# Sinkhorn of batch 0 on its own with row sums on TensorE, whole k mixes for batch 0, and fewer weight bytes in flight

## The chip, the cores and the metric

The kernel runs on one core of a Trainium2 chip. A core has five engines with a queue of instructions each, which run in order: TensorE (PE: matmuls into PSUM, and the loads of their stationary operand), VectorE (DVE), ScalarE (ACT), GpSimd (POOL) and SyncE (SP). They meet at semaphores. DMAs are issued here from POOL (loads that cast fp32 to bf16) and from SP (stores, round trips through DRAM, transposes). The metric is the device time of one execution in microseconds; lower is better.

## The reference

Four batches, 8 heads, 768 tokens in 8 blocks of 96, head dimension 64. `sort_net` gives an 8x8 matrix for each batch and head. It goes through five Sinkhorn rounds, the blocks of k and v are mixed by it, each block of q attends to the mixed block of its place, and the result goes through a bilinear feed-forward net.

```python
for _ in range(5):
    P = P - np.max(P, axis=-1, keepdims=True)
    P = np.exp(P)
    P = P / (np.sum(P, axis=-1, keepdims=True) + 1e-09)
    P = P / (np.sum(P, axis=-2, keepdims=True) + 1e-09)
k_sorted = np.einsum('bhij,bhjcd->bhicd', P, k_b)      # v in the same way
scores = scale * q_b @ k_sorted^T                      # within a block
attn = softmax(scores);  x = attn @ v_sorted           # 3072 x 512
out = ((x @ w_a) * (x @ w_b)) @ w_out                  # 512 -> 1536 -> 512
```

## The kernel before

The program is not written in the order in which it runs. Each piece of work is given to `add` with its engine, a guessed duration, what it depends on, and the buffers and PSUM banks that it takes and gives back. `Plan.solve` places the pieces by a string, `ORDER`, that names them one after another, and `emit` writes the instructions of each engine in that order. So the order on each engine is fixed, and an instruction that has to wait holds all that stand behind it on its engine. `_fill` then puts matmuls that nobody reads (line 1222) into the gaps that the plan leaves on TensorE up to 32.6 us.

What the change touches:

- **Sinkhorn** (lines 490 to 504). All 32 matrices lie on 32 partitions, 64 numbers each (`p_nat`). A round is one exponential on ACT (L492) and six DVE steps (L494 to L502): sum, reciprocal and multiply along the rows, then along the columns. The maximum is not subtracted; it cancels in the division. After five rounds the result is repeated 16 times (two copies, one on DVE and one on ACT), turned onto 128 partitions by eight matmuls (L517), and multiplied with a mask into `s_all` (L522), the matrix that mixes blocks. DVE writes `s_all` of batch 0 from PSUM; `p_col` (L533) keeps the rest, from which POOL writes `s_all` of batches 1 to 3, 2.03 us each.
- **Batch 0** goes pair of heads by pair of heads (p = 0 to 3) and in two halves of four blocks each, h = 0 for all pairs first. For each: q is transposed on TensorE (L555), k and v are mixed by matmuls with `s_all` (L582, in halves of 64 columns), v is transposed (L641), scores (L660), exponential on ACT (L665), product with v (L675), division (L681, L686), transpose of the result (L694) into `xT`. A copy out of PSUM, on ACT or DVE, follows each step on TensorE.
- **The first product**, `xT` with w_a and w_b, for batch 0 is L836; its first half needs half 0 of all four pairs. Later batches mix k and v whole (L571, or L619 for v), and use a seven-product scheme for the first product (L930). The second product is L987.
- **Loads** are issued by POOL in one fixed order: for each pair of batch 0 a half of q, k, v (loads 0 to 11), then w_a and w_b block 0, the four other halves of q, then w_a and w_b blocks 2, 1, 3 (loads 12 to 23; a block of w is 384 columns, 0.79 MB), then batch 1, w_out, and so on. `load` makes one wait for an earlier one where more than 2.8 MB would be on their way.
- **q of batch 3** (`QDMA`) is transposed by DMA, issued from SP; that of other batches on TensorE.

Of the kernel before, what the change touches and what calls it, by code (L numbers as in the profile page):

```python
# [9 lines left out]
FP32 = mybir.dt.float32  # L10
# [26 lines left out]
class Plan:  # L37
# [178 lines left out]
    def _fill(self):  # L216

        t, ops = self.warm_from.end + 0.1, sorted((o for o in self.ops if o.eng == "PE"), key=lambda o: o.start)
        for o in ops:
            if o.start > self.warm_until:  # L220
                break
            rate = 2350.0 if t > 8.5 else 1180.0
            cols = int((o.start - t - (0.25 if 8.0 < t < 13.0 else 0.1)) * rate)
            if cols >= 64:
                w = Op({"PE": 0.0}, lambda cols=cols: self.warm_fn(cols), [], [], [], 0.0, None, -1)
                w.eng, w.start, w.end = "PE", t, t + cols / rate
                self.ops.append(w)
            t = max(t, o.end)
# [4 lines left out]
    b"%z1C$e###%#'#)#+#/#-#1#5$g$i#7#;$k$m#A$o#=$q$s#G#3$u$w#C#M$y%^${#I$}#9#S%`%#%%#Y%'#O#?%)%+"  # L233
    b"#`#E%-%/#U#f%1%~%3#[#K%5#l&$%7%9#b#r%;#Q%=#W%?#x%A#h%C&@%E#n#^%G&B%I%K#t%M#d#~%O%Q%S#j$(#z"
    b"%U$.&_#p%W&a%Y$4%b%f#v%d$:%[$$&&%h&H)/&(%j&K%n%l&D&*#|%p&G&2$*&L&-&c$@&4$0%r&O&.)+$6%t&e&P"
    b"&1&g$<$&%v&R&o$B$,&j')&q$2'%$F',&T$8''&k&V'-$L$>&X&m&6&}$H)-'0&Z'#'f&8%x&^'^'h&:'b%|'j$D'a"
    b"&<'d$R$N&s'm'C&>&u'?-j'E&w'n'A'G(($J'p'J($$T'O(+$X'K(&'1'N'Q&y-r'|&|(,'3$P(#*0(/$Z*<$_*@-l"
    b"*>$V$a*2*D*B(>*8*4*F(D$]'S(@*6(J-_*H(P(F*:*T(V$c*J(L-Z(](B*V-c*P(c(R'U*L-e*](i(H*m'W(X-f*N"
    b"(N*X(_*R(T*o(o(e(0-i*u*a(u(Z-](k*Z(2({-a(a,8)%*_(q(4,:*c-v(g(6'Y(w*i(8*e(m+f'](}-p*g+i(s(:"
    b")''5*k(<*q(y)1+n'7*s'9)3)7+q)#'r)=*w';+r'=))-n-1+t't+j'v,4+l)9'x,<,7-t'z+v,>,]-3--)5,`+x,D"  # L240
    b")C,@-0,F-x*})?,C*y+z*{)I);+|+~+))O+%,H)E++)U,J,L,N)[)K+1+#)b)A+-,P+')Q)h,$)G+/,&)n)W+A+3)M"
    b")t,()^+C,*)S)z,e,,+I+5)d,g)Y*$+9)j+7,i)`**.Z+=)p,k,R.^+;)f,T+Y,V)v)l.c+?+M)|)r+[.e+O+b*&.g"
    b"+E)x,m+U/1*,.i+G/3)~,a+K,o-5,c*(+^-7+Q*..k,{-9,q,}+S.m+`,s+W-;._,.,00.+d.a/Y0*00,X/].y,2.o"
    b"0-.{,u.P,w.q-=,y,Z-?-#-A-%/^-'-C.(1E-)/`/5-+-K/7/--M.*/0/9.s.,/b.u/A.w../;-z/C/d/f.0/=/K-O"
    b"/M.}/h-Q-|/#/?.R/%-~02.T-E.$04.<-G-I06/j.&-S.V0>.>080@/E.A/O/l-U.2/G/Q.X/I.B/S-W/x0H0:/z/n"
    b".F.D/p0<0J1H/r/|/t1r/~/v.H1t.41I1v0$.J1L1z.6.L1x1M1|0B25.81~1O0D.N2$0F1U2&1Q.:1W2*2(1[1S26"
    b"202,1^221l1Y2.1`1b282:1h0L2<1j1d1n0N2>0P2B1f0V2D0X0]2@2_0c2H0_2a1q2F2Y2J2g0e0i2N0Z2c2i0o2L"
    b"2e0u0a2m2T0k2[2P2o2V0{2k0q2R2q1%0g4P0w2s4T2]2y3'0m4V2{3#2u3)0s3+4R2}2w3/1+3-4X313K0}0y4Z33"
    b"5#3M3%351'3S114]3F371-3O5%173U3;1#391=3Y3Q3A1)3=3[3C3G3W3?4e4_3j3^1/4g3`5O133z3I6L3f3h3l19"
    b"4a5Q4F151?1;3b6$4c/'0&3d4o6&3|3o5W4q/)5'5Y4H0(5)5S1A4#5[4<4J5|/+5U4L5^5d5~5+5f6(4$5-4(6*4N"  # L250
    b"5/5`4&6,4i/U4*514k574m4,5n5b4>0R594s6.4A425p/W4u534w4B0T646044664.5h55475r3p6N4D485j5t6S5l"
    b"625v6{405;6Q6}3r4:5=7#5?3t7'7%3v687)6V6T7+6:6X7>7-3x6<6_7/6Z6a73716e6]7?79756g7;6u6c776i6k"
    b"7A7C6q6>7E6s6w6m7G6@6o7K7I6y6B7M7h6D7O7c7j7Q6F7p7S7l7r7W7U7v7n7d7^7Y7x7`8*7t7[7z7|5A7f8&80"
    b"5C8(8,7~82848$5E88868.8T8:5G8<8O8V8>5I8]8@8X8_8D8B8c8Z8P8J8F8e8L8s8a8H8y8i8R8v9O8k9;4y5K8m"
    b"8x4{5M8g9'5x8o9Y4}8q6H5z8{9)8}9E6J9,9#9[9-919%9^9`9/9b9d939f9G969Q9I9l979T9h9n:u9U9j9=99:w"
    b"9r:'9K9?9p9W9t:y9A:}9x9M9v;#:{:(9z9~;'9C;79|;%;):$:*:,;-;+:.:0;:;3:4:2;/:6;5:J:8;1::;<;=:<"
    b";A;?:@:>;C:L;E:F:B;[:H;G;I:D;K:O:P;M:T:R;Q;O:V;^:X;W;S;Y:Z:o:];U:_;a;b:a;f;d:e:c;h:q;j:k:g"
    b":m;l<$;n:i;p:t<4;r;v<';t<H;|;~;x<R;z<)<J<T<L<6<W<><N<8<:<P<]<X<<<@<_<Z<B<*<b<D<c<,<F<.<0<e"
    b"<2"
)  # L260
STRASSEN_OUT = ()
QDMA = lambda b, p: b >= 3
VDMA = lambda b, p: 4 * b + p >= 6


@with_exitstack
def kernel(
# [94 lines left out]
    p_col = const.tile([P, NB, BH], BF16, name="p_col")  # L362
    p_nat = const.tile([BH, NB, NB], FP32, name="p_nat")
    ident = const.tile([P, P], BF16, name="ident")
    mask = const.tile([P, CG], BF16, name="mask")
    rsum = const.tile([BH, NB], FP32, name="rsum")
    csum = const.tile([BH, NB], FP32, name="csum")
    p_fin = const.tile([BH, NB, NB], BF16, name="p_fin")
# [9 lines left out]
    def load(fn, nbytes, deps=(), get=(), rank=0.0, many=0.0, spare=0.4):  # L378

        ds, way, behind = [d for d in deps if d is not None], nbytes, None  # L380
        for k in reversed(range(len(ld_n))):
            way += ld_n[k][1]
            if way > 2.8e6 and len(ld_n) < 24 and behind is None:
                behind = ld_i[k]
                ds.append(ld_n[k][0])
        if len(ld_n) >= 7:
            ds.append(ld_n[-7][0])
        i = add("POOL", 0.72 + many, fn, ds + ld_i[-1:], get=get, rank=rank, lat=0.0)
        i.behind = behind
        ld_i.append(i)  # L390
        d = add("DQ", nbytes / RATE, None, [i], rank=rank)
        ld_n.append((d, nbytes))
        return add("NIL", 0.0, None, [d], lat=spare)

    def sp_dma(issue, work, fn, deps, get=(), put=(), rank=0.0, lat=1.5):
        i = add("SP", issue, fn, deps, get=get, rank=rank, lat=0.6)
        return add("DH", work, None, [i], put=put, rank=rank, lat=lat)

    o_p = add("SP", 0.6, lambda: nc.sync.dma_start(
        out=p_nat, in_=sort_net.rearrange("b h i j -> (b h) i j")), lat=1.58)  # L400
# [9 lines left out]

    def pads():
# [7 lines left out]
    o_pads = add("DVE", 1.0, pads, [o_mask], rank=1)  # L419
# [68 lines left out]

    last = o_p
    o_rep = add("NIL", 0.0, None, get=[("o", "p_rep")], rank=-20)  # L490
    for it in range(5):
        last = add("ACT", 0.26, lambda: nc.scalar.activation(out=p_nat, in_=p_nat, func=AF.Exp),  # L492
                   [last], rank=-9)
        last = add("DVE", 0.21, lambda: nc.vector.reduce_sum(out=rsum, in_=p_nat, axis=AX.X),  # L494
                   [last], rank=-9)
        last = add("DVE", 0.19, lambda: nc.vector.reciprocal(out=rsum, in_=rsum), [last], rank=-9)
        last = add("DVE", 0.21, lambda: nc.vector.tensor_mul(
            out=p_nat, in0=p_nat, in1=_ap(rsum, 0, [[NB, BH], [1, NB], [0, NB]])), [last], rank=-9)
        last = add("DVE", 0.26, lambda: nc.vector.reduce_sum(
            out=csum, in_=p_nat.transpose([0, 2, 1]), axis=AX.X), [last], rank=-9)  # L500
        last = add("DVE", 0.19, lambda: nc.vector.reciprocal(out=csum, in_=csum), [last], rank=-9)
        last = add("DVE", 0.21, lambda it=it: nc.vector.tensor_mul(  # L502
            out=p_fin if it == 4 else p_nat, in0=p_nat,
            in1=_ap(csum, 0, [[NB, BH], [0, NB], [1, NB]])), [last], rank=-9)

    def p_rep(i, n):
        return _ap(buf("p_rep").bitcast(BF16), i * NB * CG, [[2 * DMODEL, BH], [NB * CG, n], [1, NB * CG]])

    reps = [add(e, d, lambda h=h, e=e: copy(
        ENG[e], p_rep(h * NBH, NBH).rearrange("p i (j c) -> p i j c", j=NB),  # L510
        _ap(p_fin, h * NBH * NB, [[NB * NB, BH], [NB, NBH], [1, NB], [0, CG]])), [last, o_rep], rank=-9)
        for h, e, d in ((0, "DVE", 0.42), (1, "ACT", 0.62))]

    def spread_ops():
        t = buf("pc")[:, 0:NB * BH].rearrange("p (j h) -> p j h", j=NB)
        for i in range(NB):
            nc.tensor.matmul(t[:, i, :], lhsT=p_rep(i, 1).rearrange("p i k -> p (i k)"),  # L517
                             rhs=ident[0:BH, 0:BH], start=True, stop=True)
    o_pc = add("PE", 0.36, spread_ops, reps + [o_ident], get=[("bank", "pc")], put=["p_rep"], rank=-9)

    def spread(eng, src, h0, n):
        eng.tensor_tensor(  # L522
            out=s_all[:, h0:h0 + n],
            in0=_ap(mask, 0, [[CG, P], [0, n], [0, NB], [1, CG]]),
            in1=_ap(src, h0, [[src.ap[0][0], P], [1, n], [BH, NB], [0, CG]]), op=ALU.mult)

    s_ok = {}
    o = add("DVE", 0.43, lambda: spread(nc.vector, buf("pc"), 0, 2), [o_pc, o_mask], put=["pc"], rank=-9)
    s_ok[0, 0] = o
    o = add("DVE", 0.95, lambda: spread(nc.vector, buf("pc"), 2, 6), [o_pc, o_mask], put=["pc"], rank=-8)  # L530
    for p in range(1, HP):
        s_ok[0, p] = o
    o_col = add("DVE", 0.43, lambda: nc.vector.tensor_copy(  # L533
        out=p_col, in_=buf("pc")[:, 0:NB * BH].rearrange("p (j h) -> p j h", j=NB)), [o_pc],
        put=["pc"], rank=-7)

    def later_spreads(rank):
        for b in range(1, B):
            o = add("POOL", 2.0, lambda b=b: spread(nc.gpsimd, p_col, b * 8, 8), [o_col, o_mask],
                    rank=rank, port=("POOL",))  # L540
# [52 lines left out]
    def mix_half(b, p, what, h, rk, after=None):  # L593
# [9 lines left out]
        return op  # L603

# [96 lines left out]
    def x_dma(b, p):  # L701
        nc.sync.dma_start_transpose(
            out=_ap(buf(("xT", b)), p * S, [[KA * S, P], [BLK, NB], [1, BLK]]),
            in_=buf(("xp", b, p)).rearrange("q i e d -> q (i e d)"))

# [455 lines left out]
    for p in range(HP):  # L1161
        rk = float(p)
        qd = q_part(0, p, 0, rk)
        kd = mix_half(0, p, "k", 0, rk)
        vd = v_part(0, p, 0, mix_half(0, p, "v", 0, rk + 0.05), rk + 0.1)
# [6 lines left out]
    for p in range(HP):  # L1172
# [3 lines left out]
        kd = mix_half(0, p, "k", 1, rk, go)  # L1176
        vd = v_part(0, p, 1, mix_half(0, p, "v", 1, rk, go), rk + 1.0)
        m = so_part(0, p, 1, True, kd, qd, vd, rk + 1.0)
        x_part(0, p, 1, m, rk + 2.0)
# [131 lines left out]
```

## Time and profile before

| | us |
|---|---|
| median of 11 runs | 245.57 (243.72 to 247.99) |
| the profiled execution | 246.36 |
| its span, first to last instruction | 244.6 |
| TensorE busy, fillers among it | 232.8 |
| fillers of line 1222 on TensorE | 10.5 |
| DVE, ACT, POOL busy | 152.3, 115.4, 110.5 |
| s_all of batch 0 begins | 14.55 |
| first product matmul begins | 30.64 |
| last matmul ends | 239.9 |

In the profile's lines, "out<-in" are the tiles that an instruction writes and reads, then come its shape and how many were merged; "[0.30 <-PE ps L582]" is idle time before it and what ended that. In a view by windows each engine has its busy time and, in brackets, its instructions; then come the granted TensorE clock, the share of time that DMA engines were busy, and the rate. In the chain of waits each line is a start, a length and the work that set the pace there; "issue" is time in which the engine waited for nothing that the profile shows.

### The profile page before, as it was taken

To read this page: it belongs to the slowest core of one execution; us is meant where nothing else is said; L and a number is where in the kernel's file an instruction comes from. 1 tells how busy PE (TensorE), PEld (TensorE's weight loads), DVE (VectorE), ACT (ScalarE), POOL (GpSimd) and SP (SyncE) were. 2 spreads that over 40 slices of the span, in tenths; PEclk is the share of its full clock that TensorE was granted. 3 is DMA by queue.
4 is the path that set the end of the run, shared out by engine and by line. 5 is a ranking of instruction groups with operands and counts; after the bars stand their busy time and mean duration, and the time that the engine had idled before them with its cause. 6 is when DMAs were issued, how large, how long until landed. Compare 5 with 4: busy or idle time off the path is not lost.

```text
span 244.6 us, 5464 instructions
## 1 busy us (share of the span) xinstructions
PE 232.8 (95%) x2180; PEld 133.3 (54%) x2196; DVE 152.3 (62%) x305; ACT 115.4 (47%) x174; POOL 110.5 (45%) x123
## 2 busy tenths in 40 slices
PE   8798799999999999999999999999999999999992
PEld 3367556676656555565564454655654455555440
DVE  6658517785656466578884464787673458877410
ACT  2267722575447351666662542666720065563110
POOL 8679997999400000539996002373440004433000
PEclk9999979999999999999999999999999999999997
DMA  5999999999995558436999699500053452000066
GB/s 67 173 198 154 190 168 181 169 148 197 201 204 115 83 141 182 89 75 76 142 148 184 128 200 151 137 3 1 0 67 64 86 118 56 0 0 3 0 129 129
DMA packets 50104, 27.88 MB, mean 114 GB/s; under 512 B 28832, under 2 KB 47008, under 8 KB 50080
## 3 DMA queue, kind: packets, MB, share of 16 engines
q0 software_dynamic: 24112, 14.16, 43.6%
q1 hardware_dynamic: 25968, 13.38, 28.0%
q8 instruction: 17, 0.28, 0.5%
q14 instruction: 7, 0.06, 0.1%
HBM read 30.29 MB, written 8.26 MB: 158 GB/s over the span
## 4 chain that ended last, share of the span: by engine, by line
PE 85%; POOL 5%; DMA 4%; issue 2%; ACT 1%; DVE 1%; SPq 0%; ACTq 0%
PE ps L930 29%; PE ps L987 24%; PE ps L836 14%; PE ps L675 3%; PE ps L660 3%; POOL hT L373 2%; PE ps L571 2%; DMA q<-in_q_dram 2%; PE ps L555 2%; PE ps L582 2%; PE ps L1222 2%; DMA vs<-vd 2%; PE ps L641 2%; POOL q L434 1%; PE ps L619 1%
## 5 line engine op out<-in xcount | busy, mean ns | idle before, releaser
L987 PE MATMUL ps<-w_out_sb,hT 128*128 128x512 bf16 x275 | 64.7, 379 | 0.9 <-issue 0.3
L373 DVE TENSOR_TENSOR f<-f,ps 128x768 f32<-128x768 f32 x54 | 49.8, 951 | 22.3 <-PE ps L930 12.2
L373 POOL TENSOR_TENSOR hT<-f 128x384 bf16<-128x384 f32 x35 | 34.4, 1001 | 49.7 <-DVE f L373 49.6
L936 ACT COPY f<-ps 128x768 f32<-128x768 f32 x54 | 42.2, 800 | 30.2 <-PE ps L930 29.9
L987 PEld LDWEIGHTS <-hT 128*128 128x128 bf16 x288 | 26.8, 98 | 29.4
L665 ACT ACTIVATE eT<-ps 96x768 bf16<-96x768 f32 x32 | 24.9, 811 | 17.1 <-PE ps L660 15.2
L373 DVE TENSOR_TENSOR hT<-a,ps 128x384 bf16<-128x384 bf16 x42 | 22.0, 549 | 16.4 <-PE ps L836 12.4
L930 PE MATMUL ps<-tx,ws_a 128*128 128x384 bf16 x108 | 26.4, 326 | 0.1
L930 PE MATMUL ps<-tx,ws_b 128*128 128x384 bf16 x108 | 26.4, 326 | 0.0
L686 DVE TENSOR_TENSOR xp<-ps,rec 96x512 bf16<-96x512 f32 x32 | 21.6, 683 | 0.7
L836 PE MATMUL ps<-xT,w_a_sb 128*128 128x384 bf16 x96 | 19.5, 343 | 0.0
L930 PEld LDWEIGHTS <-ws_b 128*128 128x128 bf16 x144 | 14.1, 98 | 9.3
L836 PE MATMUL ps<-xT,w_b_sb 128*128 128x384 bf16 x96 | 19.0, 330 | 0.0
L930 PEld LDWEIGHTS <-ws_a 128*128 128x128 bf16 x144 | 13.6, 98 | 9.9 <-ACT f L936 0.5
L847 ACT CAST a<-ps 128x768 bf16<-128x768 f32 x12 | 9.3, 800 | 20.6 <-PE ps L836 20.6
L373 POOL TENSOR_TENSOR tx<-xT 128x768 bf16<-128x768 bf16 x2 | 3.3, 1630 | 34.0 <-DMA xT<-xp 34.0
L930 PE MATMUL ps<-xT,w_a_sb 128*128 128x384 bf16 x72 | 17.6, 326 | 0.0
L930 PE MATMUL ps<-xT,w_b_sb 128*128 128x384 bf16 x72 | 17.6, 326 | 0.0
L966 ACT CAST a<-ps 128x384 bf16<-128x384 f32 x18 | 8.6, 478 | 18.9 <-PE ps L930 18.9
L316 ACT COPY o<-ps 128x512 f32<-128x512 f32 x15 | 8.6, 588 | 17.1 <-PE ps L987 16.8
L316 ACT CAST kT<-ps 128x768 bf16<-128x768 f32 (+1 forms) x19 | 12.9, 683 | 7.6 <-PE ps L571 6.6
L318 DVE COPY o<-ps 128x512 f32<-128x512 f32 x9 | 6.2, 690 | 14.2 <-PE ps L987 14.2
(95 smaller groups left out, 329.2 us busy)
## 6 DMA issues: line engine op xcount, KB each, us to landing
out_dram<-o SPq DMA_DIRECT2D x48, 128.0 KB, 2.4
k<-in_k_dram POOLq DMA_DIRECT2D x16, 192.0 KB, 6.1
v<-in_v_dram POOLq DMA_DIRECT2D x16, 192.0 KB, 6.1
vd<-vm SPq DMA_DIRECT2D x10, 192.0 KB, 2.4
vs<-vd SPq DMA_DIRECT2D x10, 192.0 KB, 3.2
q<-in_q_dram POOLq DMA_DIRECT2D x16, 96.0 KB, 5.2
w_a_sb<-in_moe_w_a_dram POOLq DMA_DIRECT2D x4, 384.0 KB, 6.2
w_b_sb<-in_moe_w_b_dram POOLq DMA_DIRECT2D x4, 384.0 KB, 6.3
```

Source lines behind the costliest of these rows:

```text
L316: nc.scalar.copy(out=out, in_=in_)
L373: ENG[eng].tensor_tensor(out=out, in0=in0, in1=in1, op=op)
L660: nc.tensor.matmul(sc[:, e, i * BLK:(i + 1) * BLK], lhsT=kT[e * D:(e + 1) * D, at:at + P], rhs=rhs, start=True, stop=True)
L665: nc.scalar.activation(out=buf(("eT", b, p, h))[:, :, 0:HB], in_=buf(("sc", b, p, h))[0:BLK, :, 0:HB], func=AF.Exp, scale=float(scale))
L675: nc.tensor.matmul(ops_[:, e, i * OW:(i + 1) * OW], lhsT=eT[:, e, i * BLK:i * BLK + P], rhs=vs[:, h * NBH + i, e * OW:(e + 1) * OW], start ...
L686: nc.vector.tensor_tensor(out=_ap(xp, h * NBH * 2 * D, [[NB * 2 * D, BLK], [D, 2], [2 * D, NBH], [1, D]]), in0=_ap(ops_, 2, [[1024, BLK], ...
L836: nc.tensor.matmul(pf[:, u, 0:HW], lhsT=w_sb[:, kc, (m + u) * P:(m + u + 1) * P], rhs=buf(("xT", b))[:, kc, t * HW:(t + 1) * HW], start=(k ...
L847: ea = add("ACT", 0.8, lambda: nc.scalar.copy(out=buf(("a", b, t, m)), in_=buf(("pf", b, t, m, "a"))[:, :, 0:HW]), [ps_["a", 1]], get=[("a ...
L930: nc.tensor.matmul(buf(key)[:, n, 0:HW], lhsT=lf(n, j), rhs=rf(j), start=start and j == 0, stop=j == 1, skip_group_check=not start)
L936: return add("ACT", 0.8, lambda: nc.scalar.copy(out=buf((name, b, g)), in_=buf(kA)[:, :, 0:HW]), [dep], get=[("f", (name, b, g))], rank=rk)
L966: e21 = add("ACT", 0.48, lambda: nc.scalar.copy(out=buf(("c21", b, g))[:, 0, :], in_=buf(kA)[:, 0, 0:HW]), [p4], get=[("a", ("c21", b, g)) ...
L987: nc.tensor.matmul(po, lhsT=hT[:, t * 2 + m // G, m % G, c * P:(c + 1) * P], rhs=w_out_sb[:, m, :], start=(m == 0), stop=(m == KO - 1), sk ...
```

## The change

1. Batch 0's Sinkhorn leaves the common chain. Its matrices lie on 64 partitions (head and row), 8 numbers each. Sums along a row are taken by the instruction that multiplies; sums along a column, over the partitions of a head, by an fp32 matmul with a mask (`m_same`) on TensorE. The row division is carried into the next exponential as a scale. The result is spread onto 128 partitions by one matmul.
2. The other three batches keep the old chain, on 24 partitions, at a late rank: their steps are put between the work on batch 0.
3. k of batch 0 is mixed whole (`WHOLE`), and copied in two halves; v stays in halves. `XDMA` is there and false.
4. Loads 12 to 23 wait where more than 2.0 MB would be on their way.
5. q of batch 2, pairs 2 and 3, is transposed by DMA as well.
6. `ORDER` is another string for the whole program, and the fillers are sized by another table of rates.

```diff
-            rate = 2350.0 if t > 8.5 else 1180.0
+            rate = 2350.0 if t > 12.4 else 1500.0 if t > 4.65 else 1180.0
...
-QDMA = lambda b, p: b >= 3
+QDMA = lambda b, p: 4 * b + p >= 10
+XDMA = lambda p: False
+WHOLE = lambda p, what: what == "k"
...
-            if way > 2.8e6 and len(ld_n) < 24 and behind is None:
+            if way > (2.8e6 if len(ld_n) < 12 else 2.0e6) and len(ld_n) < 24 and behind is None:
...
+    o_p0 = add("SP", 0.6, lambda: nc.sync.dma_start(
+        out=pa[:, 0, :], in_=sort_net[0].rearrange("h i j -> (h i) j")), lat=1.58)
     o_p = add("SP", 0.6, lambda: nc.sync.dma_start(
-        out=p_nat, in_=sort_net.rearrange("b h i j -> (b h) i j")), lat=1.58)
+        out=p_nat, in_=sort_net[1:B].rearrange("b h i j -> (b h) i j")), [o_p0], lat=1.5)
...
+    def sk_rows():
+        nc.tensor.matmul(buf(bank)[0:HN, NB:2 * NB], lhsT=m_same.rearrange("p h j -> p (h j)"),
+                         rhs=pa[:, 1, :], start=True, stop=True)
...
+    for it in range(4):
+        x = step("ACT", 0.3, lambda it=it: nc.scalar.activation(
+            out=pa[:, 1, :], in_=px if it else buf(bank)[0:HN, 0:NB], func=AF.Exp, scale=pc1), [x], lat=0.2)
+        x = step("PE", 0.12, sk_rows, [x, o_same])
+        x = step("DVE", 0.2, lambda: nc.vector.reciprocal(out=pr, in_=buf(bank)[0:HN, NB:2 * NB]),
+                 [x], put=[bank], lat=0.1)
+        x = step("DVE", 0.2, lambda: stt(px, pa[:, 1, :], 1.0, pr, ps1), [x], lat=0.02)
+        x = step("DVE", 0.15, lambda: nc.vector.reciprocal(out=pc1, in_=ps1), [x], lat=0.1)
...
+    def spread_first():
+        nc.tensor.matmul(buf("p0")[:, 0:HN], lhsT=m_rep.rearrange("p j c -> p (j c)"),
+                         rhs=p_end.rearrange("p i h -> p (i h)"), start=True, stop=True)
...
     for it in range(5):
         last = add("ACT", 0.26, lambda: nc.scalar.activation(out=p_nat, in_=p_nat, func=AF.Exp),
-                   [last], rank=-9)
+                   [last, o_p0], rank=12)
...
+    def mix_first(b, p, what, rk):
+
+        if not WHOLE(p, what):
+            return lambda h, r, after=None: mix_half(b, p, what, h, r, after)
+        pe = add("PE", 0.46, lambda: mix_pe(b, p, what),
+                 [(k_in if what == "k" else v_in)[b, p], s_ok[b, p]],
+                 get=[("pair", (what + "m", b, p))], put=[(what + "2", b, p)], rank=rk)
```

## The prediction

> **What bounds the kernel now.** I read the page first, then the windows of the first 40 us, the chain of waits, the timeline of 9 to 31 us, and last the groups of instructions by shape.
>
> ```profile
> span 244.6 us, 5464 instructions
> PE 232.8 (95%) x2180; PEld 133.3 (54%) x2196; DVE 152.3 (62%) x305; ACT 115.4 (47%) x174; POOL 110.5 (45%) x123
> ...
> PEclk9999979999999999999999999999999999999997
> ```
>
> TensorE is busy 95% of the span, so the end is set by TensorE: a change is worth what it takes from TensorE's work or from its useless time. From 33.9 us to its last matmul at 239.9 us it stands still for only 1.5 us in all. The useless time is in front. "Busy" hides it there, because the matmuls of line 1222 are fillers that nobody reads. I sorted TensorE's time by line: of the first 15.06 us, 10.34 are fillers, 2.92 idle and 1.81 useful; of 15.06 to 30.64 us, 12.79 are useful and 2.79 idle or filler.
>
> ```profile
> 14.55 1.29 DVE L522 TENSOR_TENSOR s_all<-mask,ps 128x256 bf16<-128x256 bf16 x2 [2.24 <-PE ps L517]
> ...
> 15.03 0.38 PE L582 MATMUL ps<-s_all,k 128*64 128x64 bf16 x12
> ```
>
> This is the timeline: the first useful k and v matmuls (line 582) start when s_all, the end of the Sinkhorn chain, is there. k and v of pair 0 had landed at 6.4 and 7.4 us.
>
> ```profile
> 28.50 0.22 PE ps L641 x2
> 28.72 1.75 issue
> 30.48 0.37 PE ps L641 x2
> 30.85 6.01 PE ps L836 x28
> ```
>
> The chain of waits: in the middle of one group of transposes TensorE stands still 1.75 us and waits for nothing that the profile shows. Counted in program order, this stop stands at TensorE's instruction 962; two smaller ones (0.28 us at 19.4, 0.29 us at 24.4) stand at 450 and 706. They are 256 apart, and each comes 1.3 us after the end of one packet of the "instruction" queue (packets began at 17.15, 22.08, 28.17 us; 17 of them carry 0.28 MB, so 16 KB each). I read them as TensorE out of instructions.
>
> ```profile
> 30.00:35.00 5.00, 4.53 (x20) 2.45 (x20) 0.42 (x1) 0.05 (x1) 4.98 (x6) 0.66 1.14 161
> ```
>
> The windows (the last three columns are granted clock, DMA share, GB/s): the clock is 0.50 from 30.27 to 33.69 us, right behind that stop. Matmuls filled 3.06 us of it and would need half.
>
> **The change, part by part.**
>
> *First mixing.* Before: 15.06 us. The new chain for batch 0 works on 64 partitions and 8 columns, with one small matmul on TensorE in each round in place of two DVE steps. A round now is Exp (0.26 before), matmul, reciprocal (0.19), multiply (0.21), reciprocal (0.19), with 0.12 from matmul to DVE and 0.03 to 0.04 at the other hops: about 1.2 us and the matmul, against 1.75 measured before. The trace has no matmul in fp32 and no accumulating DVE step. Below, the matmul takes 0.1 us as the shortest groups do; above, all of it eats the gain (that is a rival). But the chain is now in TensorE's queue, behind the q transposes in program order: its third row matmul behind those of pair 1 (landed 9.01), the spreading matmul behind those of pair 2 (landed 11.66, started 11.80). So: 11.80 + 0.38 transposes + 0.40 filler (858 columns at 2,130 per us, from 8 fillers in 1.83 us) + 0.1 + 0.12 + 0.42 first spread + 0.03 = 13.25. Useful work before it is three q groups, 0.53 + 0.38 + 0.38 = 1.3. Useless: 13.25 - 1.3 = 11.95 against 13.25 before (10.34 + 2.92): **1.3 gained**.
>
> *From there to the first product matmul* (line 836 before, at 30.64; 27 groups in the new order). By the old rows the new order has 10.3 us of TensorE work in front of it: whole k mixes at 0.46, half v mixes 0.31, scores 0.28, o 0.26, v transposes 0.17, x 0.17, q 0.30. The other bound is DVE, which now has two of five Sinkhorn rounds of batches 1 to 3 between its copies: two spreads 1.37, two rounds at 1.26 (0.20 + 0.19 + 0.21 + 0.26 + 0.19 + 0.21), four vs copies at 0.417, one vT and three kT at 0.556, four reciprocals 0.81, four xp at 0.682, four xT and one qT at 0.357: 13.1 us up to the last xT that the product needs. From 12.75 without a pause that is 25.9; at the 82% that DVE was busy in 14.55 to 28.60 before, 28.7. ACT's last exponential for it ends near 22.5 by the same rows. I take 26.5, nearer the low end, because the fillers that stand in this stretch are only 2,600 columns (1.2 us) and TensorE's work plus those gives 24.8. Useless: 26.5 - 13.25 - 10.3 = 2.95 against 2.79: **0.2 lost**. The product starts 4.1 us earlier because less stands ahead of it.
>
> *The instruction stop.* The new order has 805 TensorE instructions before the first product matmul, against 966. Stops 450 and 706 remain and are in the 2.95; number 962 falls behind some 28 product matmuls of 0.163 us each (4.6 us) with 3.7 us of other work. The longest refill before took 6.1 us (24.36 to 30.48), so it is covered with 2 us to spare. Without that cover it is 1.75 us again, and the half clock with it. With it the slow stretch goes: **1.5 gained** (3.06 / 2). The Trainium skill, "TensorE: Matmul & The Clock Gate" (Part 1), says the clock falls after an idle window of about 3.4 us; here a stop of 1.75 us was enough, so the row decides. By the page alone the 1.5 would not be there, and the time 1.5 higher. "Runtime: NRT & Kernel Launch" (Instruction fetch mechanics) calls crossing a 16 KiB block "mostly hidden"; the 1.75 us row differs. By the page neither order has stops, and the 0.2 lost becomes some 2 lost.
>
> *k at once*: 4 x (2 x 0.294 - 0.46) = **0.5 gained** (line 582: 4.71 us in 16 groups; line 571: 0.46). *q of batch 2, pairs 2 and 3, by DMA*: two groups of 0.46 leave TensorE, **0.9 gained**. For them SP issues two more transposes (1.3 us each, 4.9 us to landing) and POOL four q loads in place of two. SP's next vd store and output wait behind them; TensorE is 99% busy with other groups at 85 to 120 us, which hides it. If not, some 2 us each.
>
> *The remaining Sinkhorn* delays s_all of batches 1 to 3: POOL wrote it from 17.0 us, now after the spread on TensorE that stands 285 instructions behind the first product, some 14 us later, so near 41 us, and 2.03 us more on POOL behind a w_out load. Batch 1 was first mixed at 45.3. I cost it at nothing; if POOL is late, the mix holds TensorE's queue. SP now loads sort_net in two parts: batch 0 first, nothing behind it hurries.
>
> *2.0 MB on their way* instead of 2.8: of 0.79 MB weight loads two run at once, not three, and w_a and w_b of the first block wait for v of pair 2 (13.63) and k of pair 3 (15.10) in place of an issue at 11.70 and 13.92. Landings before: 18.17 and 21.39, the other six 24.82 to 36.59, 5.6 to 6.3 us after issue. Two at a time at 5.6 us a pair from 21 us on end at 37.8, and POOL's ws sums (1.65 each) stand between: 38 to 39.6. By the work in front of it, the new order needs the last block near 39. Bounds 0 (before, no product waited) and 3 us; I take **0.6 lost**, nearer zero as the first needs (30 us) meet landings of 29 to 30.
>
> Sum: 1.3 - 0.2 + 1.5 + 0.5 + 0.9 - 0.6 = 3.4 us. The profiled execution took 246.36 (span 244.6, and 1.8 around it), 0.8 over the median of the runs: it would become 243.0, and the median 245.57 becomes **242.1**.
>
> **Rivals.**
>
> *Weights decide.* For it: two loads instead of three, and the demand 4 us earlier. Against: DMA moved 190 to 200 GB/s nearly without pause either way. With 3 us of waits instead of 0.6, and the half clock back (1.5): 242.1 + 2.4 + 1.5 = **246.0**, no change.
>
> *The chain gets no shorter.* For it: unpriced fp32 matmuls and accumulations, five crossings to TensorE, fillers that take twice as long where the clock is still 0.50. Against: the wait for q decides, not the chain. First mixing again at 15.06: 242.1 + 1.8 = **243.9**.
>
> *DVE paces the stretch*, the case that ends slower. In 13 to 27 us, 2.5 us of Sinkhorn steps, each waiting for the one before and twice for ACT, stand in DVE's fixed order before copies that TensorE waits for. At 67% busy 13.1 us take 19.6, the first product is at 32.3, 5.8 later than I say: **247.9**. It decides below 71% busy (product after 31.2). For it: DVE's share over the span is 62%. Against: 82% in this stretch before.
>
> **How the numbers follow.** What this measurement can tell from no change is about 0.5%, 1.2 us: faster is below 244.3, slower above 246.8. Forecast 0.64, chain no shorter 0.14 (both faster: 0.78), weights 0.12 (same), DVE 0.10 (slower). Range: the forecast's own is 239.8 (product at 25.9, no weight waits, first mixing 12.9, 0.8 for the new order later on) to 243.6; up to 245.6 it takes in the second case and half of the first.
>
> **What would show it.** First mixing near 13.2; first product near 26.5; no TensorE stop over 1 us and clock 1.00 from 25 to 40 us; no product idle for w_a or w_b for over 0.6 us. A stop above 1.5 us anywhere in 13 to 40 us with the clock at 0.50 behind it makes it wrong, and so does a first product after 29.

## The result, and the profile after

The changed kernel takes 251.28 us (median of 12 runs, 250.19 to 252.33), the kernel before 245.42 (median of 47 runs). The ratio is 1.028, with a 95% interval of 1.026 to 1.031: slower. The forecast was 242.1. The medians are of all executions, while the ratios, here and below, leave out slow ones (those more than 1.5% above the fastest of their kernel), so the two need not agree (251.28 over 245.42 is 1.024).

The page of the changed kernel, its span, the busy time of its engines and the granted clock:

```profile
span 248.8 us, 5358 instructions
...
PE 233.9 (94%) x2115; PEld 131.4 (53%) x2131; DVE 155.8 (63%) x320; ACT 121.8 (49%) x187; POOL 112.3 (45%) x125
...
PEclk9979985999999999999999999999999999999998
```

The dip at the sixth and seventh slice (31 to 44 us) is deeper than the one of before. The timeline of the changed kernel shows what stands there (start, length, engine, line, operation; the kernel's lines have moved: L569 and L574 are the two multiplications of a round of the late Sinkhorn, L388 the sums of weight blocks, L778 the division that gives xp, L933 the first product):

```profile
13.64 0.53 PE L656 MATMUL ps<-s_all,v 128*64 128x64 bf16 x12
...
27.93 0.81 PE L933 MATMUL ps<-xT,w_a_sb 128*128 128x384 bf16 x4
...
28.43 0.21 DVE L569 TENSOR_TENSOR p_nat<-p_nat,rsum 24x64 f32<-24x64 f32 x1
...
29.32 1.65 POOL L388 TENSOR_TENSOR ws_a<-w_a_sb 128x768 bf16<-128x768 bf16 x1
...
30.40 4.63 DVE L574 TENSOR_TENSOR p_nat<-p_nat,csum 24x64 f32<-24x64 f32 x1
...
30.91 0.78 POOL L485 DMA_DIRECT2D w_b_sb<-in_moe_w_b_dram  x1
31.71 3.24 POOL L388 TENSOR_TENSOR ws_b<-w_b_sb 128x768 bf16<-128x768 bf16 x2
...
33.52 0.82 PE L933 MATMUL ps<-xT,w_a_sb 128*128 128x384 bf16 x4 [0.97 <-DMA w_a_sb<-in_moe_w_a_dram]
...
35.68 1.65 POOL L388 TENSOR_TENSOR ws_b<-ws_b,w_b_sb 128x768 bf16<-128x768 bf16 x1
35.82 1.59 DVE L569 TENSOR_TENSOR p_nat<-p_nat,rsum 24x64 f32<-24x64 f32 x1
...
37.34 0.67 DVE L778 TENSOR_TENSOR xp<-ps,rec 96x512 bf16<-96x512 f32 x1
...
38.07 1.46 PE L933 MATMUL ps<-xT,w_a_sb 128*128 128x384 bf16 x4 [3.72 <-DVE xp L778]
```

The first mixing (13.64) and the first product (27.93) are earlier than before (15.03, 30.64). TensorE first stops for 0.97 us, up to the landing of a weight block. The larger loss is on DVE: a multiplication of the late Sinkhorn took 0.21 us at 28.43, and the next, of the same size, takes 4.63 us at 30.40. It ends 0.08 us after POOL's third weight sum (34.95). The one after that, 1.59 us, ends 0.08 us after the fourth (37.33). The xp that batch 0's second half needs stands behind both in DVE's order, and TensorE stands still for 3.72 us. A half clock follows, 35.82 to 42.65 us; TensorE worked 4.58 us of it (38.07 to 42.65) and lost half, 2.3 us. In the windows of the changed kernel (columns as before: TensorE, weight loads, DVE, ACT, POOL, then clock, DMA share, GB/s) DVE looks fully busy, with two instructions:

```profile
30.00:35.00 5.00, 3.38 (x37) 1.73 (x34) 4.88 (x2) 0.94 (x2) 4.98 (x5) 1.00 1.00 136
35.00:40.00 5.00, 1.93 (x13) 0.83 (x14) 4.61 (x11) 1.30 (x3) 4.97 (x5) 0.58 0.82 109
```

The rate has fallen too: 136 and 109 GB/s, where the kernel before moved 161 and 167. Its last six weight blocks landed from 24.82 to 36.59 us, now from 28.28 to 42.72. So there were two suspects: late weights (the new limit) and multiplications that wait for POOL's sums.

### The profile page after: what moved, and what is told of

The parts are those of the page before. It is cut to its first block, busy times and chain, and to the rows that moved or that the text cites. A ratio compares the mean times of both kernels' runs of the same rounds, so it can differ in the third digit from the quotient of the medians.

```text
span 248.8 us, 5358 instructions
## 1 busy us (share of the span) xinstructions
PE 233.9 (94%) x2115; PEld 131.4 (53%) x2131; DVE 155.8 (63%) x320; ACT 121.8 (49%) x187; POOL 112.3 (45%) x125
## 4 chain that ended last, share of the span: by engine, by line
PE 85%; DMA 5%; DVE 3%; issue 3%; POOL 2%; ACT 1%; POOLq 0%; ACTq 0%; DVEq 0%
PE ps L1027 33%; PE ps L1084 25%; PE ps L933 13%; PE ps L767 3%; PE ps L752 3%; DMA q<-in_q_dram 3%; PE ps L645 2%; DMA k<-in_k_dram 2%; DVE p_nat L574 2%; PE ps L629 1%; PE ps L711 1%; PE ps L733 1%; ACT f L1033 1%; DVE p_nat L569 1%; PE ps L786 1%
## 5 line engine op out<-in xcount | busy, mean ns | idle before, releaser
L388 POOL TENSOR_TENSOR hT<-f 128x384 bf16<-128x384 f32 x35 | 34.4, 1000 | 63.0 <-DVE f L388 63.0
L388 DVE TENSOR_TENSOR f<-f,ps 128x768 f32<-128x768 f32 x54 | 50.1, 951 | 17.1 <-PE ps L1027 12.7
L1084 PEld LDWEIGHTS <-hT 128*128 128x128 bf16 x288 | 26.8, 98 | 29.5 <-issue 0.2
L757 ACT ACTIVATE eT<-ps 96x768 bf16<-96x768 f32 x32 | 25.4, 808 | 17.6 <-PE ps L752 17.2
L388 DVE TENSOR_TENSOR hT<-a,ps 128x384 bf16<-128x384 bf16 x42 | 21.8, 547 | 12.4 <-ACT a L1063 5.2
L933 PE MATMUL ps<-xT,w_a_sb 128*128 128x384 bf16 x96 | 20.4, 343 | 4.7 <-DVE xp L778 3.7
L778 DVE TENSOR_TENSOR xp<-ps,rec 96x512 bf16<-96x512 f32 x32 | 21.4, 680 | 0.6
L318 ACT COPY o<-ps 128x512 f32<-128x512 f32 x16 | 9.4, 586 | 24.4 <-PE ps L1084 21.5
L773 DVE RECIPROCAL rec<-ps 96x8 f32<-96x8 f32 x32 | 6.2, 196 | 22.6 <-PE ps L767 22.3
L933 PE MATMUL ps<-xT,w_b_sb 128*128 128x384 bf16 x96 | 19.6, 335 | 0.0
L1027 PEld LDWEIGHTS <-ws_a 128*128 128x128 bf16 x144 | 13.0, 97 | 10.8 <-DVE f L388 2.2
L1027 PE MATMUL ps<-xT,w_a_sb 128*128 128x384 bf16 x72 | 17.6, 326 | 0.0
L1027 PE MATMUL ps<-xT,w_b_sb 128*128 128x384 bf16 x72 | 17.6, 326 | 0.0
L318 ACT CAST kT<-ps 128x768 bf16<-128x768 f32 (+1 forms) x17 | 11.9, 709 | 7.5 <-PE ps L645 7.4
L1027 PEld LDWEIGHTS <-w_b_sb 128*128 128x128 bf16 x108 | 10.6, 98 | 7.0
L1027 PEld LDWEIGHTS <-w_a_sb 128*128 128x128 bf16 x108 | 9.9, 98 | 8.3 <-ACT f L1033 0.8
```

The source lines that it names most:

```text
L318: nc.scalar.copy(out=out, in_=in_)
L388: ENG[eng].tensor_tensor(out=out, in0=in0, in1=in1, op=op)
L757: nc.scalar.activation(out=buf(("eT", b, p, h))[:, :, 0:HB], in_=buf(("sc", b, p, h))[0:BLK, :, 0:HB], func=AF.Exp, scale=float(scale))
L773: nc.vector.reciprocal(out=buf(("rec", b, p, h)), in_=_ap(buf(("op", b, p, h)), 0, [[1024, BLK], [512 + D, 2], [OW, NBH]]))
L778: nc.vector.tensor_tensor(out=_ap(xp, h * NBH * 2 * D, [[NB * 2 * D, BLK], [D, 2], [2 * D, NBH], [1, D]]), in0=_ap(ops_, 2, [[1024, BLK], ...
L933: nc.tensor.matmul(pf[:, u, 0:HW], lhsT=w_sb[:, kc, (m + u) * P:(m + u + 1) * P], rhs=buf(("xT", b))[:, kc, t * HW:(t + 1) * HW], start=(k ...
```

## The experiments

| run | what it is | median us | ratio to before (95%) | longest multiplication | longest TensorE stop in 28 to 45 us |
|---|---|---|---|---|---|
| after | the change | 251.28 | 1.028 (1.026 to 1.031) | 4.63 | 3.72 |
| e1_limit | 2.8 MB again | 244.29 | 0.989 (0.979 to 0.999) | 1.25 | 0.31 |
| e2_early | multiplications forward, not far enough | 251.39 | 1.020 (1.013 to 1.027) | 5.69 | 5.09 |
| e4_both | both | 244.72 | 0.997 (0.992 to 1.001) | 0.73 | none over 0.15 |
| e5_before20 | kernel before with 2.0 MB | 249.18 | 1.015 (1.011 to 1.020) | 0.21 | 1.38 |
| e6_clear | multiplications clear of the sums, 2.0 MB | 245.44 | 1.000 (0.995 to 1.004) | 0.21 | none over 0.15 |
| e7_stt | other form of the multiplication | 251.74 | 1.024 (1.016 to 1.033) | 6.18 | 5.51 |
| e8_best | clear, 2.8 MB, more filler | 242.90 | 0.988 (0.983 to 0.994) | 0.21 | none over 0.15 |
| e9_limit24 | 2.4 MB | two runs, 242.10 and 248.69 | not settled | 0.82 | none over 0.15 |
| e10_swap | one load issue behind two sums | two runs, 246.96 and 249.77 | 1.012 (0.999 to 1.025) | 1.90 | 1.41 |
| e11_probe | e8 and ten multiplications more | two runs, 246.76 and 252.79 | not settled | 2.89 | 1.68 |
| e12_best20 | e8 with 2.0 MB | 246.50 | 1.000 (0.994 to 1.005) | 0.21 | 0.55 |
| e13_nofill | e8 without more filler | 244.79 | 0.998 (0.994 to 1.002) | 1.25 | none over 0.15 |
| e14_fill | e8 again | 242.77 | 0.986 (0.982 to 0.990) | 0.21 | none over 0.15 |
| e15_nofill | e13 again, beside it | 243.71 | 0.990 (0.984 to 0.995) | 0.21 | none over 0.15 |

The runs are from different chips, so ratios are compared, not medians. The two columns on the right are of the one profiled execution of each kernel.

**The limit alone, back to 2.8 MB** (e1_limit).

```diff
-            if way > (2.8e6 if len(ld_n) < 12 else 2.0e6) and len(ld_n) < 24 and behind is None:
+            if way > 2.8e6 and len(ld_n) < 24 and behind is None:
```

> The kernel after with the old limit of 2.8 MB for all weight loads; nothing else changes. Theory 1 (the multiplications of p_nat on DVE, two inputs in SBUF, stand still while POOL adds weights in SBUF): the weights land 3 to 6 us earlier, POOL's sums with them, and multiplications are still caught behind them: at least one of over 1.2 us, a TensorE stop of over 1.5 us between 28 and 42 us; 249 to 251 us. Theory 2 (the limit makes the weights late, and that is the loss): no TensorE stop over 0.6 us between 28 and 42 us, all clock 1.00 there; 244 to 246 us.

The time goes to 0.989: theory 2's number. But theory 1 had mispriced its own case: multiplications that POOL's sums hold up ("locked" from here on) are still there. Timeline:

```profile
25.20 1.63 POOL L388 TENSOR_TENSOR ws_a<-w_a_sb 128x768 bf16<-128x768 bf16 x1 [1.69 <-DMA w_a_sb<-in_moe_w_a_dram]
...
28.96 0.64 DVE L569 TENSOR_TENSOR p_nat<-p_nat,rsum 24x64 f32<-24x64 f32 x1
29.53 0.67 DVE L778 TENSOR_TENSOR xp<-ps,rec 96x512 bf16<-96x512 f32 x1
...
31.87 1.64 POOL L388 TENSOR_TENSOR ws_b<-ws_b,w_b_sb 128x768 bf16<-128x768 bf16 x1
...
32.40 1.20 DVE L569 TENSOR_TENSOR p_nat<-p_nat,rsum 24x64 f32<-24x64 f32 x1
```

With earlier weights POOL's first sum comes at 25.20, where no multiplication stands. The three that are caught take 0.64, 1.20 and 1.25 us, and TensorE has other work meanwhile: its longest stop is 0.31. Beside them xp, which has one input in PSUM, keeps its 0.67 us next to POOL's sum, and the column reduction, with one input, its 0.25 us at 30.13 (a sum of POOL runs to 31.12).

**The multiplications moved forward** (e2_early), and the same with 2.8 MB (e4_both). The steps of the late Sinkhorn get other starts after the plan is made; fillers and TensorE's order stay.

```diff
+AT_CHAIN = ((3, 1), (6, 3), (11, 4), (16, 3), (21, 4))
...
-                   [last, o_p0], rank=12)
+                   [last], rank=12)
...
+        for o, t in zip(self.late[sum(n for _, n in self.moved):], starts):
+            o.start = t
...
+                o.start = first.start + 1e-6 * (k + 1)
```

> The kernel after with the steps of the Sinkhorn of batches 1 to 3 moved forward on DVE and ACT: 15 of the 35 into the gaps of the chain of batch 0, the other 20 into the places of the first 20, so that all multiplications are over before POOL's first weight sum (29.3 us). Plan, fillers, TensorE's order and the weights are untouched. Theory 1: every multiplication takes 0.16 to 0.25 us, the 3.72 us stop at 38.07 is gone, the clock is 0.50 for less than 3 us after 25 us; 251.3 less 3.7 less up to 3.4 for the clock, plus 0.5 to 2 for later weights (blocks land at 33.5 to 42.7): 245 to 248 us. Theory 2: the product only waits for weights in place of xp: 249.5 to 251.5 us.

> The two edits before together: 2.8 MB for all weight loads, and the steps of the Sinkhorn of batches 1 to 3 moved forward. Theory 1: multiplications of 0.16 to 0.25 us, no TensorE stop over 0.6 us after 25 us but the one for instructions; 242 to 244.5 us, and less than the first edit alone by 4 us or more. Theory 2: the same as the first edit alone within 1 us, 244 to 246 us.

The first did not test what it should. It gained little (1.020 for 1.028), as theory 2 said, but the edit had not moved enough: one multiplication still started 0.01 us after POOL's first sum, and the last one met the fourth (1.35 us at 35.91). Timeline of e2_early:

```profile
29.18 1.65 POOL L398 TENSOR_TENSOR ws_a<-w_a_sb 128x768 bf16<-128x768 bf16 x1
...
29.19 5.69 DVE L583 TENSOR_TENSOR p_nat<-p_nat,rsum 24x64 f32<-24x64 f32 x1
...
31.56 3.23 POOL L398 TENSOR_TENSOR ws_b<-w_b_sb 128x768 bf16<-128x768 bf16 x2
```

With both edits one multiplication was caught (0.73 us); the time did not fall below that of e1_limit.

**The limit in the kernel before** (e5_before20).

```diff
-            if way > 2.8e6 and len(ld_n) < 24 and behind is None:
+            if way > (2.8e6 if len(ld_n) < 12 else 2.0e6) and len(ld_n) < 24 and behind is None:
```

> The kernel before with the limit of 2.0 MB for the weight loads from the seventh pair on (the condition of the change), and nothing else. Theory 1: the weights land some 3 to 6 us later as after the change, and the first product (30.6 us) and its followers wait for them a little: 245.4 plus 0 to 1.5 us. Theory 2: the whole loss is here already: 249 us or more.

1.5%, 3.7 us, with no lock at all. In the old order the products wait for the blocks themselves: stops of 1.38 and 1.14 us end with w_a and w_b landings at 33.44 and 36.05, and one of 1.10 with a half of q.

**The multiplications clear of the sums, with 2.0 MB** (e6_clear): six steps more go into the chain of batch 0.

```diff
-AT_CHAIN = ((3, 1), (6, 3), (11, 4), (16, 3), (21, 4))
+AT_CHAIN = ((3, 1), (6, 3), (11, 4), (16, 3), (21, 4), (26, 6))
```

> The kernel after, limit 2.0 MB kept, with the steps of the Sinkhorn of batches 1 to 3 moved forward once more: 21 of 35 stand among the chain of batch 0, the last multiplication stands in DVE's order before the copies of 24 us, ahead of POOL's first weight sum (29.3 us). Theory A (late weights alone): nothing but a stop changes its name, 250 to 252 us. Theory B (both parts, each with a price: the late weights what they cost the kernel before, 3.7 us, and the multiplication that is locked while POOL adds the rest): all multiplications 0.16 to 0.25 us, the TensorE stop of 3.7 to 5.1 us is gone and stops of about 1 us each at the products that wait for a weight block take its place, 2 to 4 us in all; 246.5 to 249 us. Theory C (the lock is all): 243 to 245 us.

Ratio 1.000, between B and C and nearer C. Timeline, and windows, of e6_clear:

```profile
25.71 0.20 DVE L588 TENSOR_TENSOR p_fin<-p_nat,csum 24x64 bf16<-24x64 f32 x1
...
28.58 1.65 POOL L398 TENSOR_TENSOR ws_a<-w_a_sb 128x768 bf16<-128x768 bf16 x1
...
30.97 3.25 POOL L398 TENSOR_TENSOR ws_b<-w_b_sb 128x768 bf16<-128x768 bf16 x2
```

```profile
30.00:35.00 5.00, 5.00 (x56) 3.19 (x55) 2.72 (x8) 2.34 (x4) 4.96 (x5) 1.00 1.02 152
35.00:40.00 5.00, 5.00 (x48) 3.09 (x46) 2.24 (x5) 2.79 (x5) 4.97 (x6) 1.00 0.73 106
```

The same sums, the same limit, a rate nearly as low as in the changed kernel, and TensorE works 10.00 of 10.00 us. Part of that may be timing: in this profile the clock rose late (20.81 us), so the first product began at 29.80 instead of 27.93, and the blocks were needed that much later. In e12_best20 below, also clear and with 2.0 MB, the product began at 26.89, and TensorE waited once for a block, 0.55 us. Against e2_early, which differs only in where steps of the late Sinkhorn stand, the ratio falls by 2.0% (4.9 us); against the changed kernel by 2.8%.

**The form of the multiplication** (e7_stt): scalar_tensor_tensor, times 1.0.

```diff
-        last = add("DVE", 0.21, lambda: nc.vector.tensor_mul(
-            out=p_nat, in0=p_nat, in1=_ap(rsum, 0, [[NB, BL], [1, NB], [0, NB]])), [last], rank=12)
+        last = add("DVE", 0.21, lambda: stt(
+            p_nat, p_nat, 1.0, _ap(rsum, 0, [[NB, BL], [1, NB], [0, NB]])), [last], rank=12)
```

> The kernel after with the ten multiplications of the Sinkhorn of batches 1 to 3 written as scalar_tensor_tensor (times 1.0) in place of tensor_tensor; two inputs in SBUF as before, same places. If the lock belongs to two inputs in SBUF: the ones beside POOL's sums again take 1 to 5 us, 250 to 252 us. If it belongs to the form tensor_tensor: all take 0.2 to 0.3 us, no stop over 2 us, 246.5 to 249 us.

Locked as before, so the form does not matter. That the inputs do is what xp and the column reduction showed in e1_limit:

```profile
28.64 6.18 DVE L530 SCALAR_TENSOR_TENSOR p_nat<-p_nat,rsum 24x64 f32<-24x64 f32 x1
...
29.12 1.65 POOL L388 TENSOR_TENSOR ws_a<-w_a_sb 128x768 bf16<-128x768 bf16 x1
30.70 0.78 POOL L485 DMA_DIRECT2D w_b_sb<-in_moe_w_b_dram  x1
31.50 3.23 POOL L388 TENSOR_TENSOR ws_b<-w_b_sb 128x768 bf16<-128x768 bf16 x2
```

**Clear, 2.8 MB, and 2,000 filler columns before the q transposes of pair 2** (e8_best), and 2.4 MB in the changed kernel (e9_limit24; its edit puts 2.4 MB for the first twelve loads as well, which had 2.8).

```diff
+            if 11.0 < o.start < 11.5:
+                cols = 2000
             if cols >= 64:
```

> The multiplications as in the run before the last (all ahead of POOL's sums), 2.8 MB for all weight loads, and 2,000 filler columns (0.9 us) in TensorE's order before the q transposes of pair 2, where TensorE stood 1.0 to 1.4 us at 11 us in four of five profiles and the clock fell to 0.50. If that stop costs the clock of the next 3.4 to 6.8 us: clock 1.00 from 5 to 40 us, first mixing still at 13.2 to 13.8, 242 to 243.5 us. If the stop is hidden by what comes after: as without the fillers, 244.3 to 244.7.

> The kernel after with 2.4 MB in place of 2.0 MB, nothing else. Three weight loads of 0.79 MB are 2.36 MB, so three may be on their way as with 2.8, where 2.0 allows two. If the number of whole loads decides: as with 2.8 MB, 243.5 to 246 us. If every byte of the limit counts: about half way, 247 to 249 us.

e8_best is 1.2% faster than the kernel before. Of the stops near 11 us that its expectation names, those of the changed kernel, e1_limit and e2_early had a half clock behind them; one of 0.94 us at 10.62 in e5_before20 and one of 1.02 us at 7.93 in e4_both had none. e9_limit24 gave 242.1 in its profiled run, with three multiplications of 0.56 to 0.82 us beside sums, and 248.7 in the other: two runs settle nothing. Its weights landed as with 2.8 MB (the third block at 24.70, before 24.82).

**One load issue moved** (e10_swap): the issue of w_b's block 1 behind the two sums of w_b.

```diff
         self._fill()
+        self.ops[74].start = self.ops[521].start + 1e-6
```

> The kernel after with one step of POOL moved: the issue of the load of block 1 of w_b, which stands between POOL's first weight sum and the next two, comes behind those two; so POOL's first three sums follow each other with nothing between. In three runs the multiplication that met the first sum was held 4.6 to 6.2 us, over the end of that sum, the issue and both following sums; in the others it got in at the next end of a sum, even between two sums in a row. If the issue between is what kept the multiplication out: it ends at the end of the first sum, 0.1 to 1.7 us long, and the later stop shrinks under 2 us; about 247 to 249 us (that block of w_b lands some 3 us later). If the state at the first sum keeps it out whatever follows: again 4 us or more, 251 to 253 us.

```profile
28.02 1.90 DVE L570 TENSOR_TENSOR p_nat<-p_nat,rsum 24x64 f32<-24x64 f32 x1
28.19 1.65 POOL L389 TENSOR_TENSOR ws_a<-w_a_sb 128x768 bf16<-128x768 bf16 x1
...
30.52 3.23 POOL L389 TENSOR_TENSOR ws_b<-w_b_sb 128x768 bf16<-128x768 bf16 x2 [0.69 <-DMA w_b_sb<-in_moe_w_b_dram]
```

The multiplication that met the first sum (it began 0.17 us before it, during a load issue) now ends with it (29.92, 0.08 after 29.84). That speaks for the issue as what prolonged the wait, but doesn't show it: POOL also paused 0.69 us behind that sum.

**Ten multiplications more, across the sums** (e11_probe, on e8_best).

```diff
+        for n in range(10):
+            w = Op({"DVE": 0.0}, self.probe, [], [], [], 0.0, None, -1)
+            w.eng, w.start, w.end = "DVE", 25.5 + n, 25.7 + n
+            self.ops.append(w)
```

> The faster kernel of the last call (multiplications ahead of POOL's sums, 2.8 MB, 2,000 filler columns) with ten multiplications more, of the form and size of those of p_nat, whose result nobody reads, at 1 us from each other in DVE's planned order from 25.5 us on, across POOL's sums. If two inputs in SBUF have to wait for a sum of POOL: those that meet a sum take until its end, 0.3 to 1.7 us each, the others 0.2; 4 to 8 us in all for the ten, TensorE stops behind DVE, 245 to 250 us. If DVE and POOL do not hold each other: ten of 0.2 us, 2 us of DVE that TensorE does not wait for, 242.9 to 244 us.

```profile
26.32 3.24 POOL L404 TENSOR_TENSOR ws_b<-w_b_sb 128x768 bf16<-128x768 bf16 x2
26.54 1.51 DVE L600 TENSOR_TENSOR extra<-p_nat,csum 24x64 f32<-24x64 f32 x1
28.43 1.22 DVE L600 TENSOR_TENSOR extra<-p_nat,csum 24x64 f32<-24x64 f32 x1
...
30.18 1.85 DVE L600 TENSOR_TENSOR extra<-p_nat,csum 24x64 f32<-24x64 f32 x1
30.30 1.65 POOL L404 TENSOR_TENSOR ws_b<-ws_b,w_b_sb 128x768 bf16<-128x768 bf16 x1
31.88 0.78 POOL L501 DMA_DIRECT2D w_b_sb<-in_moe_w_b_dram  x1
32.23 3.13 DVE L600 TENSOR_TENSOR extra<-p_nat,csum 24x64 f32<-24x64 f32 x2
...
33.37 1.66 POOL L404 TENSOR_TENSOR ws_b<-w_b_sb,ws_b 128x768 bf16<-128x768 bf16 x1
```

Four of the ten met a sum: 1.51, 1.22, 1.85 and 2.89 us (the first of the two merged at 32.23), together 7.5; the other six took 0.20 to 0.22. TensorE, idle for 0.00 us from the product to 60 us in e8_best, was idle there for 3.63, and its last matmul ended at 240.27 in place of 236.49. The clock stayed at 1.00. So the lock does this in a kernel with early weights as well, once multiplications stand among the sums.

**The limit where nothing is locked** (e12_best20, e8_best with 2.0 MB), and the pair without and with the filler.

```diff
-            if way > 2.8e6 and len(ld_n) < 24 and behind is None:
+            if way > (2.8e6 if len(ld_n) < 12 else 2.0e6) and len(ld_n) < 24 and behind is None:
```

> The faster kernel of the last call with the limit of 2.0 MB back; nothing else. It prices the limit where no multiplication meets a sum. If the limit costs no more than the 0.6 us of the prediction: 242.9 to 243.7. If the later weights cost by themselves what they cost the kernel before (3.7 us): 246 to 247. By the run with the multiplications cleared and 2.0 MB (245.4) against the one with the first part of them moved and 2.8 MB (244.7) I expect between 243.5 and 245.

> The change without its limit (2.8 MB) and with every multiplication ahead of POOL's sums; no further filler. What is left is the sum of the prediction's other terms: first mixing 1.3, stretch to the product -0.2, instruction stop and half clock 1.5, k whole 0.5, q by DMA 0.9, together 4.0 us, so 241.6 us beside 245.6 for the kernel before, a ratio of 0.984. If instead the other terms were too large as well, as the run with 2.8 MB and one multiplication caught (0.9965) says: 243.5 to 245, ratio 0.991 to 0.998. If the filler before the q transposes of pair 2 is worth something, this is slower than the kernel with it (0.988) by 0.3% or more, and the clock is 0.50 somewhere in 11 to 19 us.

> The kernel with 2.8 MB, all multiplications ahead of POOL's sums and 2,000 filler columns, timed again beside the same kernel without these columns on one chip. If the filler is worth what the two single series say (0.9882 against 0.9978): 0.5 to 1.3% faster than the one without, 242.5 to 243.5 us. If the difference lies between runs, in whether the clock rises near 6 us or only near 17 us (two of thirteen profiles), and not in the filler: the two agree within 0.4%, and both have times spread from 242 to 246 us.

> The same without the 2,000 columns. If the filler is worth something: 244.5 to 245 us again, ratio 0.995 to 0.999. If the difference lies between runs: as the kernel with the filler within 0.4%, ratio 0.988 to 0.998 for both.

With the filler the limit costs 1.1 to 1.3% (1.000 against 0.988 and 0.986), without it 0.2 to 1.0% (1.000, e6_clear, against 0.998 and 0.990): 0.4 to 3 us. The filler itself is worth 0.3% on one chip (e14_fill against e15_nofill), inside the intervals; not shown. Nor is e13_nofill clear in every execution: in its profile the clock rose late, and the last multiplication ran into POOL's first sum (24.19, 1.64 us long). TensorE lost little by it: its one stop behind it, for xp, was 0.23 us:

```profile
24.65 1.25 DVE L588 TENSOR_TENSOR p_fin<-p_nat,csum 24x64 bf16<-24x64 f32 x1
```

The page of e14_fill:

```profile
span 240.3 us, 5369 instructions
...
PE 230.5 (96%) x2118; PEld 130.3 (54%) x2134; DVE 149.7 (62%) x320; ACT 122.4 (51%) x187; POOL 112.4 (47%) x125
...
PEclk9999999999999999999999999999999999999999
```

This version, 242.77 us and 0.986 (0.982 to 0.990), beats both kernels.

## Why the prediction was wrong, point by point

- **First mixing**: forecast 13.25, 13.64 in the changed kernel, 12.70 to 14.60 in twelve of the fourteen profiles of its variants and itself. Right in the changed kernel, and q of pair 2 decided it, as said, though only just: q landed at 11.41, and the chain's last step on DVE (p_end) ended at 11.34. In the two others (e6_clear, e13_nofill) the mixing came at 15.28 and 15.29: the clock had not risen, which was part of the rival "the chain gets no shorter" in its own words ("fillers that take twice as long").
- **The stretch to the product**: 13.25 us forecast, 14.29 measured, with 2.73 useless in place of 2.95. Useful work took 11.56 instead of 10.3; a clock of 0.50 up to 15.34 lies in it. The rival "DVE paces the stretch" (product at 32.3) did not happen. Yet it came nearest to the cause: Sinkhorn steps that stand on DVE ahead of what TensorE waits for. It put the loss ahead of the product, and looked for it in DVE's share of busy time, not in steps that are held up.
- **The instruction stop**: gone, as said; but a half clock came again, behind another stop. The 1.5 us also rested on one execution of the kernel before: in e5_before20's profile the same stop took 0.66 us, and no half clock followed.
- **k whole and q by DMA**: between two profiles, before and e4_both, the mixes of lines 582 and 571 fell from 10.84 to 9.97 us of TensorE (0.9 for 0.5 forecast), and q transposes from 5.89 to 5.39 (0.5 for 0.9). That the sum, 1.4, was right is luck: the two errors cancel.
- **"The remaining Sinkhorn … I cost it at nothing"**: this step failed. It weighed only when s_all of batches 1 to 3 would come (near 41; it came at 52.76, and no mix waited for it). It didn't ask what else uses what the moved steps use. Before, all multiplications were over by 12 us, when POOL added nothing; the new order puts five of the ten behind 30 us, and three of these meet POOL's weight sums. The plan keeps sums of DVE and POOL apart by a port entry; the Sinkhorn steps have none. The cost of such meetings, by e6_clear against e2_early and the changed kernel: 2.0 to 2.8%, 5 to 7 us. In the profiled run it is the 3.72 us stop and 2.3 us of half clock: the prediction's own sign of being wrong, a stop above 1.5 us with the clock at 0.50 behind it.
- **Weights, "I take 0.6 lost"**: 0.4 to 3 us where the multiplications stand ahead of the sums; the bounds about held, the size is not settled. The last block landed at 42.72, not at 38 to 39.6, and in the changed kernel a product stood idle 0.97 us for a block, where the prediction allowed 0.6. The larger part of what the limit cost was elsewhere: later weights moved POOL's sums from 25.20 and 27.89 us (e1_limit) to 29.32 and 31.71, onto the multiplications and back to back. So either edit alone, the limit undone or the multiplications moved, brings nearly all of it back. The prediction saw the sums "stand between" the loads, and priced them only as spacing of loads.
- **The sum without these two terms** was 4.0 us (ratio 0.984). With 2.8 MB and the multiplications moved it is 0.998 and 0.990, with the filler 0.988 and 0.986: 0.5 to 3.3 us. So these five terms were probably too large together as well, though only e13_nofill's interval (0.994 to 1.002) leaves 0.984 clearly out; which of them fell short stays open. (The forecast itself is rounded: 245.57 less 3.4 is 242.17.)

The Trainium skill, "SBUF — State Buffer" (SBUF: two separate sides), states the rule that was missing from the prediction: DVE and GpSimd share a pair of SBUF ports under an exclusive lock, and a DVE operation with two inputs in SBUF has to wait for a GpSimd operation that reads SBUF. These runs agree: 0.2 us alone, 0.56 to 6.18 beside a sum, and xp with one input in PSUM not touched. The page has the lock last for one instruction; 4.63, 5.69 and 6.18 us outlast the first sum of 1.65, so there the measurement goes further.

## What to carry to other kernels

When small steps are moved in time, list what they share with the work at their new place, ports among it, and not only what they delay. A single operation of 0.2 us with both inputs in SBUF, in DVE's order ahead of something urgent, can cost what GpSimd's next sums last. And a load limit has two prices: what waits for the data, and where the work on the data moves to; undo one part at a time, since here either part alone looked like the whole cause.

## What the runs showed of the hardware

- **A locked multiplication can miss the end of a sum.** In most cases it got in at the next end of a sum, even between two sums in a row (28.96 to 29.60 in e1_limit; the boundary was near 29.5). In three profiles it was held over one sum, a load issue and two more sums (4.63, 5.69, 6.18 us). It need not begin inside a sum: the one of 6.18 us (e7_stt) began during a load issue, 0.48 us before the first sum, and in e11_probe one that began during an issue, 1.14 us before a sum, was held 2.89 us, over that issue, a second one and the sum. Other multiplications ran in 0.2 us during an issue (13.90 in e4_both, issue 13.59 to 14.33; 25.68 in e11_probe, issue 25.52 to 26.30 with a sum behind it at 26.32). What decides it stays open.
- **The clock may rise late.** In e13_nofill TensorE had no pause from 1.19 to 15.15 us (fillers among its work), and fillers of 512 columns still took 0.61 to 0.63 us at 14 us; the first record of clock 1.00 is at 16.69 (20.81 in e6_clear). In e14_fill it was 3.88, and such a filler took 0.38. The mean granted clock of both pages (0.998) does not show it, since it counts from the first record. Timelines of TensorE, first e13_nofill:

```profile
12.62 0.53 PE L646 MATMUL ps<-ident,q 64*64 64x64 bf16 x12
...
14.07 1.08 PE L1344 MATMUL ps<-ws_b 128*128 128x512 bf16 x3
15.29 0.53 PE L673 MATMUL ps<-s_all,v 128*64 128x64 bf16 x12
```

then e14_fill:

```profile
11.48 0.38 PE L648 MATMUL ps<-ident,q 64*64 64x64 bf16 x12 [0.34 <-DMA q<-in_q_dram]
...
12.39 0.63 PE L1346 MATMUL ps<-ws_b 128*128 128x512 bf16 x3
13.04 0.38 PE L675 MATMUL ps<-s_all,v 128*64 128x64 bf16 x12
```

Three fillers in 1.08 or in 0.63 us, twelve transposes in 0.53 or 0.38. Why the clock rises at one time or the other no run shows.
